# Strassen sums of the gate and up products made by TensorE inside two PSUM banks

## The chip, the cores and the metric

The kernel runs on one NeuronCore of one Trainium2 chip. The metric is device time in microseconds, the median of several executions of the whole program. Five engines take part, each with a queue of its own that it works through in order: TensorE (PE in the profile; its weight loads are PEld), VectorE (DVE), ScalarE (ACT), GpSimd (POOL) and SyncE (SP), which issues most of the loads and stores.

## The reference

```python
h   = x + irfft2(rfft2(layernorm(x)) * (w_r + 1j * w_i))       # x: 2048 x 640
z   = layernorm(h)
out = h + ((z @ w_gate) * (z @ w_up)) @ w_down                  # 640 -> 1728 -> 640
```

All of it is fp32. The change lies in the last line, in `z @ w_gate` and `z @ w_up`.

## The kernel before

The first 180 us are the spectral part (transforms as matmuls, the filter, the way back), which the change leaves alone. The rest is the feed-forward part. The 2048 tokens are worked in two blocks of 1024 (`blk` 0 and 1). The 1728 columns of gate and up are cut into 14 chunks of 128; chunks 0 to 11 go through `strassen`, chunks 12 and 13 through the plain `gu` and `gate_parts`. A block runs step `p = 6` first (chunks 12 and 13, and the operands of the Strassen products), then `p = 0` to `5`, with two chunks each: an even one (`ci == 0`) and an odd one (`ci == 1`).

A chunk computes a 2 x 2 block product: rows are gate and up, columns are the block's two halves of 512 tokens (`sb`), and the first four of the five slices of 128 along the 640 are its inner pair; the fifth slice comes as an extra term. Strassen's scheme makes seven products of it in place of eight. Each value is split into a high and a low fp32r part, and `triple` issues three matmuls of 128 x 128 x 512 for each term, so the 18 terms of a chunk are 54 matmuls. The operands on the token side are `b11`, `b21`, `b22` (slices as they are, high and low part in `xt`), and the sums `t1`, `t2` (tile `TJ["12"]`), `t3` (in `ht`'s memory) and `t4` (in `xt`), which `turn_lo`, `t_rest`, `t12` and `t34` make once per block. The weights of a chunk are `wa` (as loaded) and `ws` (sums).

Before the change each product has a PSUM bank of its own (`single()`, four banks under the tag `e`; a bank is taken at the first write and is free when its last reader is done). VectorE adds the products: `p1` is the first product, copied out by ScalarE, `u2` is o6 + p1, `u3` is u2 - o7, then `u2` gains o5 (line 805), `c22` is o5 + u3, and o3 and o4 are finished in their own banks. The finished gate and up of a half are multiplied (lines 811, 825), and ScalarE writes the high part of `h` (lines 812, 826) and VectorE the low part (lines 815, 829) for the down product. In an even chunk the down product of the step before is dealt out between the gate/up products: `some(n)` issues n of its eight token tiles (`down`: 12 matmuls of 128 x 128 x 320 into one of two banks pairs `y`, 10 where the step before is `p = 6`, and one VectorE add into `x`, line 507). `some` also pops one piece of the second block's layer norm (`fill`) with each.

The next chunk's weights are made inside the current one by `prep`: `copies` (ScalarE's 1024-wide high part of `wa`, line 699, GpSimd's low part, line 700), `sums` (GpSimd, lines 703 to 706), `high` (ScalarE, line 711) and `low` (GpSimd, line 716). `load_raw` (line 688) loads the weights after those, when `low` is done with the staging tile. `issue(wdn)` makes the two parts of the down weights (lines 462, 463). `side` holds work that is hung into a chunk at `at(0)` to `at(5)`; in block 0's last chunk (11) it makes the plain chunks' weights (`at(1)`, line 462) and normalises the eight token tiles of block 1 on ScalarE (`at(2)`, line 524), which TensorE then transposes at the start of block 1's `p = 6`.

The order in each queue is written out by hand (`tc.manual_schedule()`): an engine works in the order of the calls.

```python
order = [6, 0, 1, 2, 3, 4, 5]
steps = [(blk, p) for blk in range(2) for p in order]
# end of p == 6: the last plain chunk, then what stands ahead of chunk 0 in each queue
gu(NC - 2, 1)
gate_parts(NC - 2, 1, s12)()
for f in t34(1):
    f()
issue(wdn)
```

Of the kernel before, what the change touches and what calls it, by code (L numbers as in the profile page):

```python
# [13 lines left out]
AF = mybir.ActivationFunctionType  # L14
OP = mybir.AluOpType

P = 128
# [12 lines left out]
def view(t, offset, dims):  # L30
    return bass.AP(tensor=t.tensor, offset=t.offset + offset, ap=[list(t.ap[0])] + [list(d) for d in dims])


def f32(ap):
    return ap.bitcast(F32)
# [11 lines left out]
def tile_spectral_glu(ctx: ExitStack, tc: tile.TileContext, x, wf, wgu, wlast, wdown, wdlast,  # L47
# [8 lines left out]
    tt, act = nc.vector.tensor_tensor, nc.scalar.activation  # L56
# [9 lines left out]
    def bank(tag, bufs=2):  # L66
        return pools["a"].tile([P, 512], F32, tag=tag, name=tag, bufs=bufs)
# [4 lines left out]
    def single():  # L72
        return bank("e", 4)

    def wk(shape, name):
        return work.tile(shape, F32, tag="wk", name=name)
# [4 lines left out]
    def mmx(o, l, r, start, stop):  # L81
        nc.tensor.matmul(o, l, r, start=start, stop=stop, skip_group_check=True)  # L82
# [3 lines left out]
    def pop(n=1):  # L86
        for _ in range(n):
            if fill:
                fill.popleft()()
# [9 lines left out]
    def cut(t, o, *shape):  # L99
        v = t[:, o:o + int(np.prod(shape))]  # L100
        names = [f"d{i}" for i in range(len(shape))]
        return v.rearrange(f"p ({' '.join(names)}) -> p {' '.join(names)}", **dict(zip(names[1:], shape[1:])))
# [439 lines left out]
    TJ = {}  # L542
# [28 lines left out]

    def t_rest(j):
        b = TJ["b"][:, j].rearrange("p (a k) n -> p a (k n)", a=2)
        tt(b, b, view(TJ[j], 256, [[0, 2], [1, 256]]), op=OP.subtract)

    def t12(j):
        hi, lo = (TJ["12"][:, l].rearrange("p m k n -> p (m k) n")[:, :, j * P:(j + 1) * P] for l in range(2))
# [82 lines left out]
    for t in range(NT):  # L660
# [12 lines left out]
        if t == NT - 3:  # L673
            ht = home("qm", [P, 8192], "ht", F32R)
            hts, t3 = cut(ht, 0, 3, 2, 2, 512), cut(ht, 6144, 2, 2, 512)
# [41 lines left out]

        return copies, sums, high, low

    def triple(o, terms):  # L720
        n = len(terms)
        for i, (w, a, m) in enumerate(terms):
            whi, wlo = w[:, 0, a:a + P], w[:, 1, a:a + P]
            mmx(o, whi, m[0], i == 0, False)
            mmx(o, whi, m[1], False, False)
            mmx(o, wlo, m[0], False, i == n - 1)

    def operand(sb, k):
        return xt[:, sb, k, 0], xt[:, sb, k, 1]
# [37 lines left out]
    def strassen(c, blk, slot, ahead, downs, side):  # L767
        wa, ws = W[c]

        def some(n):  # L770
            for _ in range(n):
                if downs:
                    downs.pop(0)()
                    pop(1)

        def at(n):
            for f in side.get(n, ()):
                f()

        b11, b21, b22 = ([operand(sb, k + i) for i in range(2)] for sb, k in ((0, 0), (0, 2), (1, 2)))  # L780
        t1, t2 = ([(TJ["12"][:, 0, m, k], TJ["12"][:, 1, m, k]) for k in range(2)] for m in range(2))
        t4 = [operand(1, k) for k in range(2)]
        b5 = [operand(sb, 4) for sb in range(2)]
        hh, hl = ([hts[:, slot, sb, l] for sb in range(2)] for l in range(2))

        def product(w, a, ms, extra=()):
            o = single()
            triple(o, [(w, a + P * i, m) for i, m in enumerate(ms)] + list(extra))
            return o

        o1 = product(wa, 384, b11)
        p1, u2 = wk([P, 512], "p1"), wk([P, 512], "u2")
        act(p1, o1, AF.Copy)
        o6 = product(ws, 0, t2)
        at(0)
        if ahead:
            ahead[0]()
            ahead[1]()
        tt(u2, o6, p1, op=OP.add)  # L799
        at(1)  # L800
        o7 = product(ws, 640, [(t3[:, k, 0], t3[:, k, 1]) for k in range(2)])
        u3, c22 = wk([P, 512], "u3"), wk([P, 512], "c22")
        tt(u3, u2, o7, op=OP.subtract)
        o5 = product(ws, 256, t1, [(wa, 896, b5[1])])
        tt(u2, o5, u2, op=OP.add)  # L805
        tt(c22, o5, u3, op=OP.add)
        some(2)
        at(2)
        o3 = product(ws, 896, b22, [(ws, 512, b5[1])])
        tt(o3, o3, u2, op=OP.add)  # L810
        tt(o3, o3, c22, op=OP.mult)  # L811
        act(hh[1], o3, AF.Copy)  # L812
        at(3)
        some(1)
        tt(hl[1], o3, f32(hh[1]), op=OP.subtract)
        some(1)
        o2 = product(wa, 0, b21, [(wa, 256, b5[0])])
        if ahead:
            ahead[2]()
            ahead[3]()  # L820
        tt(p1, o2, p1, op=OP.add)
        o4 = product(wa, 640, t4, [(wa, 896, b5[0])])
        some(1)
        tt(o4, o4, u3, op=OP.add)
        tt(o4, o4, p1, op=OP.mult)  # L825
        act(hh[0], o4, AF.Copy)  # L826
        at(4)
        some(2)
        tt(hl[0], o4, f32(hh[0]), op=OP.subtract)
        some(8)  # L830
        at(5)

# [4 lines left out]
    for n, (blk, p) in enumerate(steps):  # L837
        if p == 6:
            s13, s12 = count % 3, (count + 1) % 3
            if blk == 0:  # L840
# [16 lines left out]
                for j in range(4):  # L857
                    t_rest(j)
# [8 lines left out]
            else:  # L867
# [21 lines left out]
                for j in range(4):  # L889
                    t1s[j][0]()  # L890
                    t_rest(j)
# [25 lines left out]
        for ci in range(2):  # L917
            c = 2 * p + ci
            side = {}
            ahead = None  # L920
            if c < 11:
                ahead = prep(c + 1, blk)
                side[5] = [lambda c=c: load_raw(c + 2)] if c < 10 else []
            if ci == 0:
                side[3] = [lambda wdn=wdn: issue(wdn)]
            if c == 11 and blk == 0:
                pop(len(fill))
                dj = load_direct(1, [wk([P, D], "draw"), stage[:, 0:640], stage[:, 640:1280]])
                side[1] = [lambda: issue(dj[0]), lambda: issue(dj[1]), lambda: load_raw(0)]

                def low(ks):
                    for k in ks:
                        if k == 0:
                            TJ["z"] = home("qr", [P, 6, D], "zt")
                        normalise(8 + k, TJ["z"][:, k] if k < 6 else wk([P, D], "z"))

                side[2] = [lambda: low(range(8))]
            strassen(c, blk, slots[ci], ahead, downs if ci == 0 else [], side)
            count += 1
# [134 lines left out]
```

## Time and profile before

| | us |
|---|---|
| median of 3 runs | 723.58 (723.57 to 725.05) |
| profiled execution, span from first to last instruction | 723.0 |
| of it TensorE busy | 703.4 |
| VectorE busy | 467.6 |
| ScalarE busy | 252.6 |
| GpSimd busy | 293.3 |
| mean granted TensorE clock | 0.993 of full speed |

The span is that of one profiled execution; the median of the runs is 0.6 us above it. In the timeline, instructions of one kind that follow each other are merged into a row, with their count at the end; a bracket gives the engine's idle time before the row and what ended it. L82 is the one line that issues all matmuls of the feed-forward part, so they are told apart by their tiles: `e<-xt,wst`, `e<-t,wst` and `e<-ht,wst` are gate/up products of the Strassen chunks, `e<-xt,wdir` those of the plain chunks, `y<-wd,ht` the down product.

### The profile page before, as it was taken

The page shows a single profiled execution, that of the slowest core. Times are in us where ns is not written, and L with a number is a line of the kernel's source. Part 1 is how long each engine was busy: PE and PEld are TensorE (multiplying, and loading weights), DVE is VectorE, ACT ScalarE, POOL GpSimd, SP SyncE. Part 2 cuts the span into 40 slices and gives each one's busy share as a digit, 9 for nine tenths or more (in the row PEclk, how much of TensorE's full clock was granted, in tenths as well). Part 3 has the DMA queues.
Part 4 walks back from the last instruction along what each step waited for, and adds up shares of the span by engine and source line. Part 5 has one row for each costly group of instructions (what it writes and reads, how often), then busy time and mean ns, then how long its engine had stood idle before and what let it go on. Part 6 is the DMA issues. An engine that isn't in the chain of part 4 may idle for free.

```text
span 723.0 us, 10130 instructions
## 1 busy us (share of the span) xinstructions
PE 703.4 (97%) x3892; PEld 624.1 (86%) x3892; DVE 467.6 (65%) x810; ACT 252.6 (35%) x481; POOL 293.3 (41%) x270
## 2 busy tenths in 40 slices
PE   7899998999999999999999999999999999999998
PEld 7888997987878898989898888888898989898987
DVE  7968887698976665656555557565555555555454
ACT  4756666355532222122222256232222221222200
POOL 3310114332144545546464624055545446464600
PEclk9899999999999999999999999999999999999999
DMA  9405765000221212121010222311212121110203
GB/s 339 166 1 163 232 203 192 1 0 1 73 74 37 73 37 73 37 73 38 19 65 26 92 74 92 127 37 37 73 36 74 38 73 36 37 63 10 73 1 146
DMA packets 20928, 55.06 MB, mean 76 GB/s; under 512 B 2320, under 2 KB 6928, under 8 KB 20880
## 3 DMA queue, kind: packets, MB, share of 16 engines
q1 hardware_dynamic: 20304, 52.70, 21.4%
q0 software_dynamic: 288, 1.48, 0.6%
q8 instruction: 31, 0.51, 0.3%
q10 hardware_dynamic: 288, 0.23, 0.1%
q14 instruction: 17, 0.14, 0.1%
HBM read 49.16 MB, written 5.24 MB: 75 GB/s over the span
## 4 chain that ended last, share of the span: by engine, by line
PE 82%; DVE 11%; issue 4%; ACT 2%; DMA 1%; POOL 0%; DVEq 0%; POOLq 0%; ACTq 0%
PE e L82 43%; PE y L82 26%; PE re L82 2%; PE im L82 2%; PE u L340 2%; PE eo L82 2%; DVE fold L190 2%; DVE fold L195 1%; DVE x L507 1%; PE im L389 1%; PE im L390 1%; PE ir L381 1%; ACT zt L524 1%; DVE bits L214 1%; DVE x L509 1%
## 5 line engine op out<-in xcount | busy, mean ns | idle before, releaser
L82 PE MATMUL e<-xt,wst 128*128 128x512 f32 x864 | 207.0, 390 | 0.9 <-DVE ht L653 0.9
L82 PE MATMUL y<-wd,ht 128*128 128x320 f32 x1312 | 201.7, 310 | 1.6 <-DVE x L507 1.1
L82 PEld LDWEIGHTS y<-wd,ht 128*128 128x128 f32 x1312 | 195.3, 188 | 6.4 <-DVE x L507 2.7
L82 PEld LDWEIGHTS e<-xt,wst 128*128 128x128 f32 x864 | 160.6, 188 | 32.9 <-DVE ht L653 1.3
L507 DVE TENSOR_TENSOR x<-y,x 128x640 f32<-128x640 f32 x119 | 97.7, 822 | 73.6 <-PE y L82 73.3
L700 POOL TENSOR_TENSOR wst<-raw,wst 128x1024 fp32r<-128x1024 f32 x24 | 58.0, 2418 | 168.5 <-ACT wst L699 168.5
L716 POOL TENSOR_TENSOR wst<-raw,wst 128x896 fp32r<-128x896 f32 (+1 forms) x46 | 64.9, 1433 | 22.3 <-ACT wst L711 22.3
L82 PE MATMUL e<-t,wst 128*128 128x512 f32 x288 | 73.2, 389 | 0.0
L463 POOL TENSOR_TENSOR wd<-draw,wd 128x640 fp32r<-128x640 f32 x28 | 44.4, 1607 | 56.9 <-ACT wd L462 42.5
L812 ACT ACTIVATE ht<-e 128x512 fp32r<-128x512 f32 x24 | 14.4, 599 | 151.3 <-DVE e L811 151.3
L82 PEld LDWEIGHTS e<-t,wst 128*128 128x128 f32 x288 | 54.0, 188 | 11.7 <-ACT u L650 0.5
L826 ACT ACTIVATE ht<-e 128x512 fp32r<-128x512 f32 x24 | 14.4, 599 | 114.0 <-DVE e L825 114.0
L82 PE MATMUL e<-xt,wdir 128*128 128x512 f32 x180 | 41.9, 391 | 1.1 <-DVE q L493 1.1
L82 PEld LDWEIGHTS e<-xt,wdir 128*128 128x128 f32 x180 | 33.4, 188 | 8.3 <-ACT xt L546 1.3
L699 ACT ACTIVATE wst<-raw 128x1024 fp32r<-128x1024 f32 x24 | 25.4, 1060 | 33.8 <-DMA raw<-in_wgu_dram 33.8
L206 PE MATMUL im<-bits,fold 128*128 128x128 f32 x192 | 30.9, 306 | 6.1 <-DVE fold L195 1.8
L82 PE MATMUL e<-ht,wst 128*128 128x512 f32 x144 | 36.5, 389 | 0.0
L805 DVE TENSOR_TENSOR u<-e,u 128x512 f32<-128x512 f32 x24 | 16.6, 692 | 29.5 <-PE e L82 29.4
L206 PEld LDWEIGHTS im<-bits,fold 128*128 128x128 f32 x192 | 26.6, 209 | 9.5 <-POOL fold L180 4.2
L799 DVE TENSOR_TENSOR u<-e,p 128x512 f32<-128x512 f32 x24 | 16.6, 692 | 24.0 <-PE e L82 23.0
L408 POOL CAST qr<-bits 1x128 fp32r<-1x128 f32 x16 | 4.5, 282 | 68.0 <-DVE qr L405 68.0
L82 PEld LDWEIGHTS e<-ht,wst 128*128 128x128 f32 x144 | 27.0, 188 | 5.6
(185 smaller groups left out, 1049.2 us busy)
## 6 DMA issues: line engine op xcount, KB each, us to landing
raw<-in_wgu_dram SPq DMA_DIRECT2D x24, 640.0 KB, 3.9
wts<-in_wf_dram SPq DMA_DIRECT2D x16, 644.0 KB, 4.1
draw<-in_wdown_dram SPq DMA_DIRECT2D x24, 320.0 KB, 4.7
x<-in_x_dram SPq DMA_DIRECT2D x16, 320.5 KB, 5.9
out_dram<-x SPq DMA_DIRECT2D x15, 320.0 KB, 2.2
bits<-in_mm_dram SPq DMA_DIRECT2D x32, 128.0 KB, 4.1
raw<-in_wgu_dram SPq DMA_DIRECT2D x4, 320.0 KB, 4.2
draw<-in_wdlast_dram SPq DMA_DIRECT2D x4, 320.0 KB, 2.9
```

What stands on the lines that cost most here:

```text
L82: nc.tensor.matmul(o, l, r, start=start, stop=stop, skip_group_check=True)
L190: lambda: nc.vector.scalar_tensor_tensor(view(f, 320, [[161, 2], [1, 161]]), view(XP[t], 0, [[320, 2], [1, 161]]), SC[t][1], view(XP[t], 6 ...
L206: nc.tensor.matmul(pm[:, k * P:(k + 1) * P], l, c, start=n == 0, stop=n == len(ls) - 1)
L340: nc.tensor.matmul(ps[h][:, 0:NQ], WM[g][0][:, h], T[g][:, h], start=True, stop=True)
L463: los.append(lambda r=r, a=a, b=b: engine.tensor_tensor(w[:, 1, a:b], r, f32(w[:, 0, a:b]), op=OP.subtract))
L507: tt(xv, ps[:, :, 0:320], xv, op=OP.add)
L699: act(wa[:, 0], stage[:, 0:1024], AF.Copy)
L700: nc.gpsimd.tensor_tensor(wa[:, 1], stage[:, 0:1024], f32(wa[:, 0]), op=OP.subtract)
L716: ptt(ws[:, 1, o:o + b - a], stage[:, a:b], f32(ws[:, 0, o:o + b - a]), op=OP.subtract)
L799: tt(u2, o6, p1, op=OP.add)
L805: tt(u2, o5, u2, op=OP.add)
L812: act(hh[1], o3, AF.Copy)
```

## The change

The seven products stay, and so do their 54 matmuls; the signs of the `t3` operand are turned (`t_rest` makes d - b for the first half of the tile and b - d for the second, in two half-size VectorE operations instead of one). Three banks per chunk are named at its start: `p11`, `acc_a` and `p53`. In `acc_a` the products b11, t2, t3 and t4 are accumulated one after the other (`start=False` leaves what is in the bank), and what stands there between them is read out: ScalarE copies b11's product to `p1` and the sum with t2 to `u2`, VectorE adds the sum with t3 to `m5`, and after t4 the bank holds the finished sum. In `p53` the t1 product is copied to `m5` by ScalarE and b22 is added on top. The product of b21 moves from the sixth to the second place. VectorE's operations fall from eleven to seven per chunk, ScalarE's rise from three to five (without the weights). The down steps of an even chunk, two, two and four before, become two, one, two and three.

```diff
@@ -571,7 +571,9 @@
 
     def t_rest(j):
         b = TJ["b"][:, j].rearrange("p (a k) n -> p a (k n)", a=2)
-        tt(b, b, view(TJ[j], 256, [[0, 2], [1, 256]]), op=OP.subtract)
+        d = TJ[j][:, 2:4].rearrange("p k n -> p (k n)")
+        tt(b[:, 0], d, b[:, 0], op=OP.subtract)
+        tt(b[:, 1], b[:, 1], d, op=OP.subtract)
 
     def t12(j):
         hi, lo = (TJ["12"][:, l].rearrange("p m k n -> p (m k) n")[:, :, j * P:(j + 1) * P] for l in range(2))
@@ -717,11 +719,11 @@
 
         return copies, sums, high, low
 
-    def triple(o, terms):
+    def triple(o, terms, start=True):
         n = len(terms)
         for i, (w, a, m) in enumerate(terms):
             whi, wlo = w[:, 0, a:a + P], w[:, 1, a:a + P]
-            mmx(o, whi, m[0], i == 0, False)
+            mmx(o, whi, m[0], start and i == 0, False)
             mmx(o, whi, m[1], False, False)
             mmx(o, wlo, m[0], False, i == n - 1)
 
@@ -783,50 +785,47 @@
         b5 = [operand(sb, 4) for sb in range(2)]
         hh, hl = ([hts[:, slot, sb, l] for sb in range(2)] for l in range(2))
 
-        def product(w, a, ms, extra=()):
-            o = single()
-            triple(o, [(w, a + P * i, m) for i, m in enumerate(ms)] + list(extra))
-            return o
-
-        o1 = product(wa, 384, b11)
-        p1, u2 = wk([P, 512], "p1"), wk([P, 512], "u2")
-        act(p1, o1, AF.Copy)
-        o6 = product(ws, 0, t2)
+        p11, acc_a, p53 = single(), single(), single()
+
+        def product(o, w, a, ms, extra=(), start=True):
+            triple(o, [(w, a + P * i, m) for i, m in enumerate(ms)] + list(extra), start)
+
+        product(acc_a, wa, 384, b11)
+        p1, u2, m5 = (wk([P, 512], n) for n in ("p1", "u2", "m5"))
+        act(p1, acc_a, AF.Copy)
+        product(p11, wa, 0, b21, [(wa, 256, b5[0])])
         at(0)
         if ahead:
             ahead[0]()
             ahead[1]()
-        tt(u2, o6, p1, op=OP.add)
+        tt(p1, p11, p1, op=OP.add)
         at(1)
-        o7 = product(ws, 640, [(t3[:, k, 0], t3[:, k, 1]) for k in range(2)])
-        u3, c22 = wk([P, 512], "u3"), wk([P, 512], "c22")
-        tt(u3, u2, o7, op=OP.subtract)
-        o5 = product(ws, 256, t1, [(wa, 896, b5[1])])
-        tt(u2, o5, u2, op=OP.add)
-        tt(c22, o5, u3, op=OP.add)
+        product(acc_a, ws, 0, t2, start=False)
+        act(u2, acc_a, AF.Copy)
+        product(p53, ws, 256, t1, [(wa, 896, b5[1])])
+        act(m5, p53, AF.Copy)
         some(2)
         at(2)
-        o3 = product(ws, 896, b22, [(ws, 512, b5[1])])
-        tt(o3, o3, u2, op=OP.add)
-        tt(o3, o3, c22, op=OP.mult)
-        act(hh[1], o3, AF.Copy)
+        product(acc_a, ws, 640, [(t3[:, k, 0], t3[:, k, 1]) for k in range(2)], start=False)
+        tt(m5, acc_a, m5, op=OP.add)
+        some(1)
+        product(p53, ws, 896, b22, [(ws, 512, b5[1])], start=False)
+        tt(p53, p53, u2, op=OP.add)
+        tt(p53, p53, m5, op=OP.mult)
+        act(hh[1], p53, AF.Copy)
         at(3)
-        some(1)
-        tt(hl[1], o3, f32(hh[1]), op=OP.subtract)
-        some(1)
-        o2 = product(wa, 0, b21, [(wa, 256, b5[0])])
+        some(2)
+        tt(hl[1], p53, f32(hh[1]), op=OP.subtract)
         if ahead:
             ahead[2]()
             ahead[3]()
-        tt(p1, o2, p1, op=OP.add)
-        o4 = product(wa, 640, t4, [(wa, 896, b5[0])])
+        product(acc_a, wa, 640, t4, [(wa, 896, b5[0])], start=False)
         some(1)
-        tt(o4, o4, u3, op=OP.add)
-        tt(o4, o4, p1, op=OP.mult)
-        act(hh[0], o4, AF.Copy)
+        tt(acc_a, acc_a, p1, op=OP.mult)
+        act(hh[0], acc_a, AF.Copy)
         at(4)
-        some(2)
-        tt(hl[0], o4, f32(hh[0]), op=OP.subtract)
+        some(1)
+        tt(hl[0], acc_a, f32(hh[0]), op=OP.subtract)
         some(8)
         at(5)
```

## Rows read from the trace of the kernel before

**Rows 1.** The page's busy us, share of the span and instructions of TensorE.

```profile
PE 703.4 (97%) x3892; PEld 624.1 (86%) x3892; DVE 467.6 (65%) x810; ACT 252.6 (35%) x481; POOL 293.3 (41%) x270
```

**Rows 2.** The chain of waits (start us, us, what), one pair of chunks.

```profile
267.67 18.39 PE e L82 x81
...
286.05 3.52 PE y L82 x24
```

**Rows 3.** Timeline, block 0's first chunk: start us, us, engine, line, operation.

```profile
202.90 1.65 PE L82 MATMUL e<-xt,wst 128*128 128x512 f32 x6 [0.88 <-DVE ht L653]
...
203.97 0.58 ACT L650 ACTIVATE u<-e 128x512 f32<-128x512 f32 x1
...
206.86 1.35 ACT L462 ACTIVATE wd<-draw 128x640 fp32r<-128x640 f32 x2
...
208.12 0.59 ACT L793 ACTIVATE p<-e 128x512 f32<-128x512 f32 x1
...
211.24 2.02 PE L82 MATMUL y<-wd,ht 128*128 128x320 f32 x12 [0.37 <-POOL wd L463]
...
213.10 2.23 PE L82 MATMUL e<-xt,wst 128*128 128x512 f32 x9
...
227.19 1.74 PE L82 MATMUL y<-wd,ht 128*128 128x320 f32 x10 [0.44 <-DVE x L507]
```

**Rows 4.** Timeline, first chunk of block 1, same columns.

```profile
475.01 1.52 PE L82 MATMUL e<-xt,wst 128*128 128x512 f32 x6
...
476.01 0.60 ACT L652 ACTIVATE ht<-e 128x512 fp32r<-128x512 f32 x1 [2.06 <-DVE e L651]
...
478.71 0.59 ACT L793 ACTIVATE p<-e 128x512 f32<-128x512 f32 x1
...
497.76 1.47 PEld L82 LDWEIGHTS y<-wd,ht 128*128 128x128 f32 x10 [0.31 <-DVE x L507]
```

**Rows 5.** Timeline, last chunk of block 0 and block change, same columns.

```profile
421.99 1.55 PE L82 MATMUL e<-xt,wst 128*128 128x512 f32 x6
...
427.65 4.99 ACT L524 ACTIVATE zt<-x,b,r 128x640 f32<-128x640 f32 x6 [1.60 <-PE e L82]
...
434.17 0.58 ACT L812 ACTIVATE ht<-e 128x512 fp32r<-128x512 f32 x1
...
437.44 0.60 ACT L826 ACTIVATE ht<-e 128x512 fp32r<-128x512 f32 x1 [2.69 <-DVE e L825]
...
441.51 2.02 PE L82 MATMUL y<-wd,ht 128*128 128x320 f32 x12 [0.50 <-DVE x L507]
```

**Rows 6.** Timeline of VectorE ahead of block 0's first chunk; line 803's group.

```profile
196.93 0.43 DVE L706 TENSOR_TENSOR raw<-raw 128x256 f32<-128x256 f32 x1
...
197.28 2.49 DVE L574 TENSOR_TENSOR bt<-bt,tj 128x512 f32<-128x512 f32 x4
...
L803 DVE TENSOR_TENSOR u<-u,e 128x512 f32<-128x512 f32 x24 | 16.5, 688 | 14.3 <-PE e L82 13.7 <-POOL wd L463 0.5
```

**Rows 7.** Timeline, an odd chunk and the next's start; GpSimd's line 716.

```profile
267.51 1.55 PE L82 MATMUL e<-xt,wst 128*128 128x512 f32 x6
...
278.88 2.82 POOL L716 TENSOR_TENSOR wst<-raw,wst 128x896 fp32r<-128x896 f32 x2 [2.21 <-ACT wst L711]
...
281.44 0.60 ACT L826 ACTIVATE ht<-e 128x512 fp32r<-128x512 f32 x1 [2.33 <-DVE e L825]
...
L716 POOL TENSOR_TENSOR wst<-raw,wst 128x896 fp32r<-128x896 f32 x23 | 48.8, 2124 | 22.3 <-ACT wst L711 22.3
```

**Rows 8.** Stretches: us, busy us (instructions) by engine, granted clock, DMA share, GB/s.

```profile
120.00:125.00 5.00, 2.90 (x21) 2.13 (x19) 3.76 (x9) 3.04 (x8) 2.59 (x6) 1.00 0.12 46
...
125.00:130.00 5.00, 4.61 (x22) 4.64 (x22) 1.01 (x3) 0.44 (x1) 1.23 (x4) 0.66 0.00 0
...
202.00:203.00 1.00, 0.12 (x2) 0.11 (x1) 1.00 (x3) 0.00 (x0) 0.00 (x0) 1.00 0.75 113
```

## The prediction

> **What bounds the kernel now.** I read the page's busy times first: TensorE is busy for 703.4 of the 723.0 us span [rows 1], so an edit can win only where TensorE stands still, and lose wherever it makes TensorE wait. The chain of waits says the same for the Strassen part: for pages on end it names TensorE alone. There 81 gate/up matmuls take 18.39 us, 0.227 each, and 24 down matmuls 3.52, 0.147 each [rows 2]. A pair of chunks (108 of the first, 96 of the second) is 38.6 us with no gap, and neither VectorE nor ScalarE stands on that chain. Then I read the timeline at the seams, where TensorE does wait: the first Strassen chunk of each token block [rows 3, 4], the change from block 0 to block 1 [rows 5], and the spectral part, which the change does not touch.
>
> **The change, part by part.**
>
> *Matmuls.* Seven products before and after, 18 terms of 3 matmuls, 54 in all. TensorE's work stays, so in the steady part the gain is nil. Per chunk VectorE loses four of its eleven operations (0.688 us each [rows 6], 24 x 4 x 0.688 = 66 us) and ScalarE gains two copies (0.59 each, as the one that is there [rows 3]; 28 us). VectorE is not on the chain, so its 66 us buy nothing by themselves.
>
> *New waits in a steady chunk.* TensorE now adds into a bank that ScalarE or VectorE has just read, four times per chunk, and all its later matmuls queue behind each wait. A copy starts about 0.2 us after its product and takes 0.6, so 0.8 us are needed. The product put between has at least 6 matmuls, 1.36 us, so about 0.5 us is to spare. What can use it up is ScalarE's queue. At the start of an even chunk the first copy stands behind the activation that ends the odd chunk before it; that activation starts at 281.44 today [rows 7], the copy 0.5 later. Its multiply now comes after the other half's subtraction, but one add is gone, so both start some 0.05 us later; the copy is done at 282.6, and the third product starts at 279.80 + 15 x 0.2275 = 283.2 (279.80 is 54 matmuls after the chunk's start [rows 7]). Covered by 0.6.
>
> *The moved weights.* The products that end the first half of h move from the 36th to the 45th matmul of an odd chunk, 2.05 us later; behind that activation in ScalarE's queue stand the high parts of the next weights, behind those GpSimd's low parts, behind those SP's next weight load, behind that the next 1024-wide weight copy. GpSimd's low part starts at 278.88 and its first piece lasts 2.12 [rows 7]; it becomes 280.93 to 283.05. Its reader, the third matmul of the sum product, moves as well, from the 9th matmul of the next chunk to the 18th: 283.67. Before and after some 0.6 us (0.4 if the weights are wanted one matmul ahead). The load lands about 2 us later and holds the u copy to 289.2, while two down steps put its reader at 290.1. I take 0 for the 24 steady chunks.
>
> The Trainium skill (Perfetto Trace Analysis, section Matmuls) speaks against this change: independent matmul groups should rotate through different banks, so that the copy out of one overlaps the next group. By that alone all four waits of 0.8 would be bare, 24 x 4 x 0.8 = 77 us by the rows; the product put between them is why I do not take it.
>
> *First chunk of block 0.* Here ScalarE is late. In its queue ahead of the first product's copy stand the gate parts of chunk 12, a T34 activation and two weight activations; the copy runs from 208.12 to 208.71, 5.2 us after the first matmul at 202.90 [rows 3]. Nobody minded: the first bank was wanted only by the fifth product. Now the third product wants it after 15 matmuls, 3.4 us. VectorE feeds this queue (TensorE's own wait at 202.90 is for it), and it gets eight half-size subtractions for four: 2.49 us become 8 x 0.35 = 2.8 by the spacing of the 256-wide operations at 196.93 and 197.28, at most 8 x 0.43 = 3.4 [rows 6]. So +0.3 (0 to 0.95). Then: first product 203.20 to 204.57; second product in the bank whose reader ended at 204.56, now 204.86, so 204.9 to 206.95; copy done at 209.0; third product 209.1; 30 matmuls done at 209.1 + 15 x 0.2275 = 212.5, two down steps (20 x 0.147) 215.45. Today 27 matmuls and the two steps are done at 213.10 [rows 3], with three more 213.8. Loss 1.7. This has already swallowed the 0.37 wait for the down weights at 211.24, since the first down step comes 3 matmuls later. Against it the 0.44 wait at 227.19 goes: there two down steps' adds, an add, a multiply and a third add were in one row on VectorE, of which the add leaves and the down steps are spread; with the refilling of the weights 0.5. Net +1.2.
>
> *First chunk of block 1.* The same queue: first matmul at 475.01, copy at 478.71 to 479.30; its head, the activation at 476.01, waits for the last product before, so it can't be earlier [rows 4]. The third product would start at 478.42; it waits until 479.35, with the weights' refill 1.0 us. VectorE's extra 0.3 is hidden, since it waits for TensorE here. The 0.31 wait at 497.76 goes. Net +0.7.
>
> *Block change.* In block 0's last chunk ScalarE normalises eight tiles, from 427.65 [rows 5], as soon as the T operands were read. Now two copies come before them: the second can start 0.2 after 30 matmuls, 421.99 + 6.83 + 0.2 = 429.0, so the eight start at 429.5. They last 6.5 (434.17 - 427.65), so h's first activation moves from 434.17 to 436.0. After it: subtraction 0.7, one multiply 0.7 (it was add, add, multiply), second activation at 438.05 instead of 437.44. All transposed copies follow it, then the down step's add that TensorE waits for at 441.51: +0.6. Bounds 0 (something else is late by as much) and 1.85 (the whole delay).
>
> *End.* The last chain is add, multiply, activation, subtraction; now the first half's chain ends 2.05 us nearer the end, and multiply, activation and subtraction of the second follow. By the same durations it ends within 0.1 us. 0.
>
> Sum: 1.2 + 0.7 + 0.6 = 2.5 us on the profiled span of 723.0, 725.5. The median of the runs, 723.58, lies 0.6 above that span: **726.1 us**, 0.35% slower.
>
> **The rivals.**
> 1. *The clock falls.* From 120 to 125 us TensorE stood idle for 2.1 of 5 us in short gaps; from 125 to 130 its granted clock was 0.66 on the mean, that is 3.4 us at its lower level, 1.2 GHz, and 1.7 lost [rows 8]. In block 0's first chunk it would now stand idle 1.2, 0.3 and 2.1 us within 7. For it: about as idle a stretch. Against: today's 0.88 wait at 202 left the clock at 1.00 [rows 8]. 726.1 + 1.7 = 727.8. The Trainium skill (TensorE: Matmul & The Clock Gate, section on psum-queue depth-cycling) describes it: short idles between matmul groups, caused by cycling through banks, make the clock swing.
> 2. *Odd chunks miss their weights.* The 0.4 us to spare is the only cover where an odd chunk is followed by an even one, 10 times. If the new copies push the low parts back by 0.3 more than that, 10 x 0.3 = 3.0: 729.1.
> 3. *Banks are handed out in strict turn.* Then the second product of a chunk gets the bank that the chunk before reads last (the activation at 281.44 and a subtraction behind it, 282.8) and not at 281.2: 10 x 1.6 = 16, 742. Against: at 202.90 the first product waits for the gate bank of chunk 12, which is the bank freed longest ago and not the next in turn.
> 4. *Not slower: the block starts are covered.* If ScalarE reaches the first copy within 3.4 us of the first matmul, neither wait appears, and what is left is -0.37 - 0.44 - 0.31 + 0.6 = -0.5: 723.1. It decides at that one point. For: nothing but the written order puts four activations ahead. Against: the rows show them in that order in both blocks, at 3.7 and 5.2 us.
> 5. *Faster.* As 4, and the remaining waits at the seams go too (0.88 at 202.90, 0.50 at 441.51 instead of +0.6): 721.1. Nothing in the rows speaks for it.
>
> **How the numbers follow.** Chances: forecast 0.46 (own range 725.1 to 727.2, from the bounds of the subtractions and of the block change), clock 0.22, weights 0.08, banks 0.03, covered 0.14, faster 0.07. A measurement can tell about 0.2%, 1.45 us: 722.1 to 725.0 counts as the same. Slower: 0.46 x 0.92 + 0.22 + 0.08 + 0.03 = 0.75; same 0.18; faster 0.07. The range leaves out the faster case, the banks, most of the weights and a little of the covered case: 724.0 to 728.8.
>
> **What would show it.** Right: the steady pair still 38.6 us; a wait of TensorE for ScalarE's first copy of about 2 us near 207 and 1 us near 478; the waits at 211.24, 227.19 and 497.76 gone; the wait at 441.5 about 0.6 later; VectorE's busy time down by some 65 us, ScalarE's up by 28. Wrong: waits for a copy or for low parts in every second chunk (rivals 2, 3), a granted clock of 0.5 near 209 (rival 1), or a first copy that comes before the 15th matmul (rival 4).

## The result and the profile after

The changed kernel takes 727.17 us (median of 7 runs, 725.52 to 727.35); the kernel before, run beside it, 723.85 (723.41 to 725.11). The ratio over all runs is 1.0035, 95% interval 1.0024 to 1.0047: slower by about a third of a per cent, as forecast, at a forecast of 726.1 us. The times of both kernels lie in two groups some 1.6 us apart (before 723.4 to 723.9 and 725.1, after 725.5 to 725.9 and 727.2 to 727.4), and as the median before fell into the lower group and the median after into the upper, the 3.3 us between the medians overstate the change, which costs 2.1 to 2.2 us group by group. Stage by stage, by the starts of matmuls in the two traces (stage A's start is that of its row in the timeline, the others are the chain's, which lie 0.16 us behind the row in both kernels):

| stage | begins with | before us | after us | difference | forecast |
|---|---|---|---|---|---|
| A: end of block 0's `p = 6` and its first Strassen chunk | 45 plain-chunk matmuls at 191.53; 190.00 | 37.40 | 38.46 | +1.06 | +1.2 |
| B: ten steady chunks of block 0 | 228.93; 228.46 | 193.22 | 193.20 | 0.0 | 0 |
| C: chunk 11 and the block change | 422.15; 421.66 | 32.59 | 33.11 | +0.52 | +0.6 |
| D: block 1's `p = 6` and first chunk | 454.74; 454.77 | 44.76 | 45.53 | +0.77 | +0.7 |
| E: ten steady chunks of block 1 | 499.50; 500.30 | 193.10 | 193.20 | +0.1 | 0 |
| F: last chunk and end | 692.60; 693.50 | 30.4 | 30.3 | -0.1 | 0 |

A, C and D make 2.35, forecast 2.5. The page of the changed kernel, against [rows 1]: VectorE 61 us less (467.6 to 406.5), ScalarE 27 more (252.6 to 279.3), TensorE the same work.

```profile
PE 701.4 (97%) x3892; PEld 620.4 (86%) x3892; DVE 406.5 (56%) x722; ACT 279.3 (39%) x529; POOL 293.0 (40%) x270
```

The chain of waits of the changed kernel, one pair of steady chunks, which answers to [rows 2]:

```profile
228.46 19.07 PE e L82 x84
...
261.82 5.28 PE y L82 x36
267.10 19.07 PE e L82 x84
```

The pair is 267.10 - 228.46 = 38.64 us, as before, with TensorE alone on the chain. Where TensorE waits in the feed-forward part is seen in the list of its waits (waiting line, releaser's line, us in total, times, longest):

```profile
PE e L82 <- ACT p L795: 2.6, 2, 1.8
...
PE e L82 <- DVE ht L655: 1.2, 1, 1.2
...
PE y L82 <- DVE x L507: 1.0, 1, 1.0
...
PE y L82 <- ACT ht L815: 0.5, 1, 0.5
```

These are the lines that bear on the change: two waits for the first product's copy (line 795), none for the other two new copies (804, 806) in the 24 chunks of this execution; the wait for the down weights [rows 3] and those at 227.19 and 497.76 [rows 3, 4] are not in the list any more. The timeline of block 0's first chunk, against [rows 3]:

```profile
201.64 4.03 PE L82 MATMUL e<-xt,wst 128*128 128x512 f32 x15 [1.16 <-DVE ht L655]
...
204.16 0.60 ACT L654 ACTIVATE ht<-e 128x512 fp32r<-128x512 f32 x1 [0.87 <-DVE e L653]
204.66 1.05 ACT L586 ACTIVATE xt<-bt 128x1024 fp32r<-128x1024 f32 x1
...
205.60 1.35 ACT L462 ACTIVATE wd<-draw 128x640 fp32r<-128x640 f32 x2
...
206.86 0.58 ACT L795 ACTIVATE p<-e 128x512 f32<-128x512 f32 x1
...
207.49 3.06 PE L82 MATMUL e<-t,wst 128*128 128x512 f32 x12 [1.82 <-ACT p L795]
```

ScalarE works without a pause from 204.16 to the copy: T34's activation and the down weights' two stand ahead of it, and the third product waits 1.82 us. In block 1, against [rows 4], the same, with 0.78:

```profile
478.74 0.59 ACT L795 ACTIVATE p<-e 128x512 f32<-128x512 f32 x1
...
479.37 3.02 PE L82 MATMUL e<-t,wst 128*128 128x512 f32 x12 [0.78 <-ACT p L795]
```

The block change, against [rows 5]:

```profile
428.58 0.60 ACT L806 ACTIVATE m<-e 128x512 f32<-128x512 f32 x1 [1.50 <-PE e L82]
429.07 4.98 ACT L524 ACTIVATE zt<-x,b,r 128x640 f32<-128x640 f32 x6
...
435.58 0.58 ACT L815 ACTIVATE ht<-e 128x512 fp32r<-128x512 f32 x1
...
436.21 1.28 PE L82 MATMUL y<-wd,ht 128*128 128x320 f32 x6 [0.53 <-ACT ht L815]
...
436.80 0.69 DVE L824 TENSOR_TENSOR e<-e,p 128x512 f32<-128x512 f32 x1
...
437.52 0.60 ACT L825 ACTIVATE ht<-e 128x512 fp32r<-128x512 f32 x1 [1.36 <-DVE e L824]
...
441.59 2.02 PE L82 MATMUL y<-wd,ht 128*128 128x320 f32 x12 [1.03 <-DVE x L507]
```

The normalisations stand behind the copy of line 806, and h's first activation, behind them, is late. Part of this comes back before h's second activation (line 825, before the change 826): in the kernel before, two adds stood between them on VectorE, beside a subtraction and a multiply that both kernels have. They were

```profile
435.39 0.68 DVE L821 TENSOR_TENSOR p<-e,p 128x512 f32<-128x512 f32 x1
435.99 0.69 DVE L824 TENSOR_TENSOR e<-e,u 128x512 f32<-128x512 f32 x1
```

### The profile page after: what moved, and what is told of

The parts are those of the page before. It is cut to its first block, busy times and chain, and to the rows that moved or that the text cites. A ratio compares the mean times of both kernels' runs of the same rounds, so it can differ in the third digit from the quotient of the medians.

```text
span 723.8 us, 10024 instructions
## 1 busy us (share of the span) xinstructions
PE 701.4 (97%) x3892; PEld 620.4 (86%) x3892; DVE 406.5 (56%) x722; ACT 279.3 (39%) x529; POOL 293.0 (40%) x270
## 4 chain that ended last, share of the span: by engine, by line
PE 81%; DVE 13%; ACT 3%; issue 2%; DMA 1%; DVEq 0%; ACTq 0%
PE e L82 42%; PE y L82 27%; PE re L82 2%; PE im L82 2%; PE u L340 2%; PE eo L82 2%; DVE fold L190 1%; DVE fold L195 1%; PE im L389 1%; PE im L390 1%; PE ir L381 1%; ACT zt L524 1%; DVE bits L214 1%; DVE x L509 1%; DVE q L492 1%
## 5 line engine op out<-in xcount | busy, mean ns | idle before, releaser
L82 PE MATMUL e<-xt,wst 128*128 128x512 f32 x864 | 209.2, 390 | 1.2 <-DVE ht L655 1.2
L82 PE MATMUL e<-t,wst 128*128 128x512 f32 x288 | 69.5, 390 | 2.6 <-ACT p L795 2.6
L810 DVE TENSOR_TENSOR m<-e,m 128x512 f32<-128x512 f32 x24 | 16.6, 691 | 54.7 <-PE e L82 54.3
L801 DVE TENSOR_TENSOR p<-e,p 128x512 f32<-128x512 f32 x24 | 16.6, 692 | 39.5 <-PE e L82 38.5
L813 DVE TENSOR_TENSOR e<-e,u 128x512 f32<-128x512 f32 x24 | 16.8, 700 | 29.1 <-PE e L82 29.1
```

Of the source, the lines that this page charges most:

```text
L801: tt(p1, p11, p1, op=OP.add)
L810: tt(m5, acc_a, m5, op=OP.add)
L813: tt(p53, p53, u2, op=OP.add)
```

## The experiments

**1. The down weights behind the copy.** Is it ScalarE's order that costs, at the two first chunks? The first hunk is the end of `p == 6`.

```diff
-            issue(wdn)
+            held = wdn
...
+                if p == 0:
+                    side[0] = [lambda held=held: issue(held)]
```

> The changed kernel, but in the first chunk of each block ScalarE makes the two down weight parts after the first product's copy instead of before it. Theory (the loss at the first chunks is the place of that copy in ScalarE's queue): the copy comes 1.3 us earlier. Block 0: TensorE's wait for it falls from 1.82 to about 0.5 us; block 1: from 0.78 to nothing. Sum -2.2 us against the changed kernel, ratio to the kernel before 1.0005 instead of 1.0035. The down weights are ready at about 210.4 by the time of the changed kernel's trace, their reader comes at 210.9, so no wait there. Rival (the wait belongs to the bank sharing itself, not to the queue): the waits stay, ratio 1.0035.

Measured: 723.36 us (12 runs), ratio 0.9997 (0.9988 to 1.0006). Stage A is 37.18 us (from 38.46), D 44.45 (from 45.53), 2.36 us together where 2.2 were expected; B and C stay (193.20, 33.12). The copy now comes at 205.68, right behind T34's activation:

```profile
205.68 0.59 ACT L795 ACTIVATE p<-e 128x512 f32<-128x512 f32 x1
...
206.16 1.36 ACT L462 ACTIVATE wd<-draw 128x640 fp32r<-128x640 f32 x2
...
206.32 1.89 PE L82 MATMUL e<-t,wst 128*128 128x512 f32 x7 [0.57 <-ACT p L795]
```

The wait falls from 1.82 to 0.57, and A by 1.28; the one of 0.78 in block 1 is gone, and D is 1.08 shorter. It is ScalarE's order, and the wait that goes altogether, block 1's, gives back 0.3 us more than the list shows for it (experiments 4 and 6 say the same).

**2. VectorE makes the copies in chunk 11 of block 0.** Is the block change late because of the two copies ahead of the normalisations?

```diff
+        copy = nc.vector.tensor_copy if (blk, c) == (0, 11) else lambda o, i: act(o, i, AF.Copy)
...
-        act(u2, acc_a, AF.Copy)
+        copy(u2, acc_a)
...
-        act(m5, p53, AF.Copy)
+        copy(m5, p53)
```

> The changed kernel, but in block 0's chunk 11 the copies u2 and m5 are made by VectorE, so that ScalarE can start normalising when the T operands were read. Theory: the eight normalisations start about 1.5 us earlier (near 427.6 where they start at 429.07), h's first activation near 434.1 instead of 435.58, and TensorE's wait before the third down step at the block change falls from 1.03 to about 0.5 us; -0.5 us in all, ratio 1.0028. That is less than the timing can tell, so the trace decides. Rival (another chain holds that down step): its wait stays near 1.0 although the normalisations start earlier.

Measured: 724.59 us (11 runs), ratio 1.0018 (1.0009 to 1.0028). Stage C is 31.88: 1.23 us less than the change's 33.11, where 0.5 were expected, and 0.7 less than before's 32.59. The timeline:

```profile
427.86 4.99 ACT L524 ACTIVATE zt<-x,b,r 128x640 f32<-128x640 f32 x6 [2.23 <-PE e L82]
...
434.38 0.58 ACT L816 ACTIVATE ht<-e 128x512 fp32r<-128x512 f32 x1
...
436.32 0.60 ACT L826 ACTIVATE ht<-e 128x512 fp32r<-128x512 f32 x1 [1.36 <-DVE e L825]
...
440.38 1.88 PE L82 MATMUL y<-wd,ht 128*128 128x320 f32 x11 [0.74 <-DVE x L507]
```

The normalisations start 1.21 earlier than in the changed kernel, and the end of the stage moves by all of it: the place was right and the size was not. TensorE's wait for line 507 falls only to 0.74, but the one of 0.53 before it is gone as well. The end of the stage hangs on h's second activation: the row in which TensorE waits for line 507 starts 4.07, 4.07 and 4.06 us after it in the kernel before, the changed kernel and here. Counted from the start of chunk 11 (421.99, 421.50 and 421.51), h's first activation starts at 12.18, 14.08 and 12.87, the second at 15.45, 16.02 and 14.81. So the change delays the first by 1.90 us, 1.2 of it by the two copies and 0.7 because the T operands' last product now ends three matmuls later; the two adds that VectorE no longer makes in between give back 1.33, and 0.57 is left. With the copies on VectorE, the second activation comes 0.64 earlier than before, and C is 0.71 shorter.

**3. The old scheme at the seams alone.** Chunk 0 of both blocks and chunk 11 of block 0 in the scheme of before, the other 21 in the new one; the turned sign of `t3` and with it the half-size subtractions stay.

```diff
+    def strassen_apart(c, blk, slot, ahead, downs, side):
...
+        tt(u3, u2, o7, op=OP.add)
...
-            strassen(c, blk, slots[ci], ahead, downs if ci == 0 else [], side)
+            scheme = strassen_apart if c == 0 or (blk, c) == (0, 11) else strassen
+            scheme(c, blk, slots[ci], ahead, downs if ci == 0 else [], side)
```

> The changed kernel, but chunk 0 of both blocks and chunk 11 of block 0 keep seven products in banks of their own, in the old order; the other 21 chunks accumulate in two banks. Theory (all of the loss lies at these three seams): TensorE's waits for copies vanish, and what is left against the kernel before is the doubled half-size subtractions, 0.3 us; ratio 1.0000 to 1.0010. Rival (the steady chunks lose a little each, 21/24 of the loss): ratio about 1.003.

Measured: 723.74 us (11 runs), ratio 1.0005 (0.9996 to 1.0014). Stages A, C, D are 37.64, 32.60, 44.75 (before 37.40, 32.59, 44.76), B 193.25. The change's loss in A, C and D is that of three chunks, and the ten steady chunks of stage B cost nothing. Those of stage E cost 0.8 us in this execution (193.97, after 193.20), by one wait for a copy, which had been expected to vanish:

```profile
674.25 1.06 ACT L701 ACTIVATE wst<-raw 128x1024 fp32r<-128x1024 f32 x1 [6.70 <-DMA raw<-in_wgu_dram]
...
675.85 1.66 PE L82 MATMUL e<-ht,wst 128*128 128x512 f32 x6 [0.50 <-ACT u L804]
```

The load of the next weights was issued at 668.87 and let ScalarE begin 5.4 us later, against 3.9 to 4.7 in the nine other even chunks of B and E; the copy of `u2` stood behind it. What is left in A, 0.24 us, fits the half-size subtractions (forecast 0.3), the only part of the change that stays there.

**4. No product between.** The t2 product stands right behind b11's in the same bank, in every chunk.

```diff
         product(acc_a, wa, 384, b11)
...
         act(p1, acc_a, AF.Copy)
+        product(acc_a, ws, 0, t2, start=False)
+        act(u2, acc_a, AF.Copy)
...
-        product(acc_a, ws, 0, t2, start=False)
-        act(u2, acc_a, AF.Copy)
```

> The changed kernel, but the product that shares the first product's bank comes right behind it in every chunk, with no other product between. Theory (the product put between is what hides the copy): TensorE now waits for the copy in every chunk. Where ScalarE is free the wait is 0.2 + 0.6 + 0.05 = 0.85 us; where an even chunk follows an odd one, the copy stands behind the activation of h and the wait is about 1.5; in the first chunks of the blocks it grows by 2. 12 x 0.85 + 10 x 1.5 + 4 + the 2.6 that are there = about 30 us more than the changed kernel less these 2.6, so 753 (750 to 758). Rival (TensorE's queue hides a wait of that size): under 730.

Measured: 760.63 us in a single run, span 758.8, 35.0 above the changed kernel's; 753, that is 29.2 above its span, was expected. The list of waits and a steady chunk's row:

```profile
PE e L82 <- ACT p L795: 27.5, 24, 4.2
```

```profile
317.94 1.65 PE L82 MATMUL e<-t,wst 128*128 128x512 f32 x6 [0.69 <-ACT p L795]
...
331.68 1.77 PE L82 MATMUL e<-t,wst 128*128 128x512 f32 x6 [1.21 <-ACT p L795]
```

The 0.69 is an odd chunk's, where the copy finds ScalarE free; the 1.21 is an even one's, where the activation of line 825 stands ahead of it. Two things make the loss larger than expected. A pair loses 41.23 - 38.64 = 2.59 us where 0.85 + 1.5 = 2.35 was expected; the waits shown are only 1.90, but each costs 0.35 more than it shows. And the clock falls. Stretches of block 0's first chunk (us, busy us and count of PE, PEld, DVE, ACT, POOL, granted clock, DMA share, GB/s):

```profile
202.00:204.00 2.00, 1.44 (x6) 0.83 (x5) 1.34 (x3) 1.07 (x2) 0.00 (x0) 1.00 0.96 387
204.00:206.00 2.00, 0.00 (x0) 0.00 (x0) 1.08 (x3) 1.69 (x3) 0.00 (x0) 1.00 0.51 201
206.00:208.00 2.00, 0.36 (x1) 0.36 (x2) 1.11 (x1) 1.59 (x3) 1.45 (x1) 0.68 0.00 0
208.00:210.00 2.00, 2.00 (x6) 1.54 (x6) 0.00 (x0) 0.00 (x0) 2.00 (x2) 0.50 0.00 0
```

TensorE waits 4.2 us there; the granted clock falls to 0.50, which is 1.2 GHz, and the next 24 matmuls take 8.51 us in the chain instead of 24 x 0.2275 = 5.46. Of the 3.05 more, 0.33 is what the changed kernel's chain shows behind such a wait too (3.74 us for 15 matmuls, 3.41 at 0.2275); 2.7 are lost to the clock.

**5. All three seams mended.** Experiment 2's copies by VectorE, and both the down weights and T34's last activation (with VectorE's subtraction that belongs to it) behind the first copy.

```diff
-            for f in t34(1):
-                f()
-            issue(wdn)
+            held = t34(1) + [lambda wdn=wdn: issue(wdn)]
...
+                if p == 0:
+                    side[0] = held
```

> The changed kernel with all three seams mended: in block 0's chunk 11 VectorE makes the two copies, and both the last T34 activation and the down weights' activations are issued behind the first Strassen product's copy of each block. My theory (the loss is ScalarE's queue at three places and nowhere else): against the changed kernel 1.3 us come back at block 0's first chunk with the weights moved alone; the T34 activation moved too takes most of the 0.57 us wait that was left there (0.5); 0.7 at block 1's; 1.2 at the block change. Sum about 3.5 us off the changed kernel: 723.7 less, counted like with like against the kernel before, some 1.2 us faster than before, ratio about 0.998 (0.997 to 0.9995), and no wait of TensorE for line 795's copy in the trace. Rival (the remedies overlap, or the moved activations make the second or fourth product late instead): ratio 1.000 or above, with a new wait near 206 to 215 us or near 476 to 485 us.

Measured: 721.77 us (6 runs, 721.61 to 721.82), ratio 0.9970 (0.9958 to 0.9982) to the kernel before, which took 723.57 beside it: faster than both kernels, by 0.3% than the one before. Stages A to D are 36.79, 193.20, 31.89, 44.45. The list of TensorE's waits has no line for the three copies any more; what is left of those above is

```profile
PE e L82 <- DVE ht L655: 1.2, 1, 1.2
...
PE y L82 <- DVE x L507: 0.7, 1, 0.7
```

and there is a new wait of 0.2 us for the down weights, which now come later. The span is 720.0, 3.8 below the changed kernel's, where 3.5 were expected.

**6. The second copy three times over.** How much more would the cover bear?

```diff
-        act(m5, p53, AF.Copy)
+        for _ in range(3):
+            act(m5, p53, AF.Copy)
```

> The changed kernel with the M5 copy (the second copy out of a shared bank) done three times over in every chunk; the result is the same. It tests the size of the cover. My theory: the product put between needs 6 matmuls, 1.36 us; from the product's end to the release one copy needs 0.2 + 0.6, three need 0.2 + 0.6 + 2 x 0.49 + 0.05 = 1.83. So each chunk in which no down step stands there (12 of 24) waits 0.47 us, with the refill of the weights about 0.6, and the block change moves by about 1 us: 727.2 + 12 x 0.6 = 734, with 12 waits of about 0.5 us for line 806's copy; the other 12, which have two down steps (3.6 us) more of cover, none. Rival (ScalarE's queue, not the cover, sets what can be borne): the second copy delays the next weights' high parts as well, and waits for weights appear, 740 or more. Rival (the release is earlier than the copy's end): under 730.

Measured: 736.73 us in a single run, span 735.0, 11.2 above the changed kernel's; about 7 was expected. The waits, and the rows of an odd chunk (no down step) and of the even one behind it:

```profile
PE e L82 <- ACT m L807: 7.1, 12, 0.6
```

```profile
274.96 1.86 ACT L807 ACTIVATE m<-e 128x512 f32<-128x512 f32 x3 [1.44 <-PE e L82]
...
276.88 7.79 PE L82 MATMUL e<-xt,wst 128*128 128x512 f32 x33 [0.59 <-ACT m L807]
...
291.42 1.55 PE L82 MATMUL e<-ht,wst 128*128 128x512 f32 x6
```

Twelve waits of 0.59, in the chunks without a down step there, and none in the other twelve: as the first theory has it. The price is higher: a pair is 39.54 us instead of 38.64, so 0.90 for a wait shown as 0.59, again 0.31 more; 12 x 0.90 = 10.8, and the block change adds 0.4. With one copy the same arithmetic leaves 1.36 - 0.85 = 0.5 us of cover unused.

**7. The new order without the change.** Does the mended kernel's gain come from the change, or only from the order of ScalarE's work? The kernel before, with the edit of experiment 5 in `p == 6` and `side[0]`, and nothing else.

> The kernel before, with the last T34 activation and the down weights' activations issued behind the first Strassen product's copy, as in the mended kernel, and nothing of the change. It asks whether the 1.8 us that the mended kernel is faster than before come from the change or from the new order. My theory (from the change: its fewer VectorE operations take away waits of 0.44, 0.68 and 0.31 us for VectorE at the three seams): here those waits stay, and the down weights come 0.5 us later behind the copy, so that the wait for them of 0.37 us near 211 becomes about 0.8. 723.6 + 0.4 = 724.0, ratio 1.0005 (1.000 to 1.0015). Rival (the order gives the gain): about 721.8, ratio 0.9975, with none of the waits for VectorE left.

Measured: 724.31 us (11 runs), ratio 1.0000 (0.9991 to 1.0009). Stages A to D are 37.85, 193.21, 32.61, 44.99. The waits for VectorE stay, and those for the down weights grow (0.37 in one wait before):

```profile
208.92 1.15 PE L82 MATMUL y<-wd,ht 128*128 128x320 f32 x6 [0.25 <-POOL wd L463]
210.44 2.02 PE L82 MATMUL y<-wd,ht 128*128 128x320 f32 x12 [0.37 <-POOL wd L463]
...
226.40 1.73 PE L82 MATMUL y<-wd,ht 128*128 128x320 f32 x10 [0.44 <-DVE x L507]
```

So the order alone gains nothing: the timing shows no difference, and the stages are 0.45 (A), 0.02 (C) and 0.23 us (D) longer than before, 0.7 in all, where the down weights come later. Against before, the mended kernel gains 0.61 in A, 0.70 in C and 0.31 in D, 1.6 in all. In C it is VectorE's two adds (experiment 2), in D the wait of 0.31 for VectorE at 497.76 [rows 4] is gone. In A the wait of 0.44 for VectorE is gone and the one for the down weights, which are GpSimd's, falls from 0.37 to 0.2, while the wait for line 655 is 0.28 longer. Against this kernel the mended one gains 1.06, 0.72 and 0.54, 2.3 in all; it differs from this kernel by the change and by VectorE's copies in chunk 11, which only the change has.

## Why the prediction held

*Steady chunks, 0.* Held: the pair is 38.64 before and after, and in experiment 3 the ten of stage B cost nothing, those of stage E 0.8 in one wait behind a late weight load, which the forecast did not have. The Trainium skill (Perfetto Trace Analysis, section Matmuls) has independent groups rotate through banks; by that alone the four waits would have been bare. They are covered, because another bank's product stands between, and the copies overlap it, as the page would have it; experiment 4 shows what one of the four costs when it is bare in every chunk, 35 us with the clock's part.

*Moved weights, 0.* Held: in the changed kernel the odd chunk's low part starts 13.41 us after its chunk (280.35 - 266.94), before 11.37 [rows 7]; the 2.04 are the 2.05 of the forecast, and TensorE has no wait for them.

*First chunk of block 0, +1.2.* Measured +1.06. The third product starts at 207.49, which is 209.02 on the scale of before (the stage begins 1.53 earlier); forecast 209.1. The half-size subtractions' 0.3 is 0.24 in experiment 3 (the wait of TensorE that follows them, 0.88 before, is 1.16), and experiment 1 returns 1.28 with the weights alone.

*First chunk of block 1, +0.7.* Measured +0.77. Third product at 479.37, forecast 479.35. The wait shown is 0.78 and gives back 1.08 in experiment 1; the forecast had 0.93 and under 0.1 for refilling the weights, for which no row stood: the runs show about 0.3 behind a wait, and the two misses cancel.

*Block change, +0.6.* Measured +0.52, and the steps come where they were put: on the scale of before (0.49 later) the normalisations at 429.56 (429.5), h's first activation at 436.07 (436.0), the wait ends at 442.08 (441.51 + 0.6). The working holds too: the forecast took 1.85 of delay, less what VectorE's fewer operations give back before h's second activation (438.05 instead of 437.44); measured are 1.90, and 438.01 on the scale of before. What was mis-sized is experiment 2's expectation, which had 0.5 for the two copies; they cost 1.2.

*The median.* The sum came out well because two wrong numbers in it cancel. One is the 0.6 us between span and median. In the eight other executions profiled here the run's own time lies 1.7 to 2.0 above its span (725.52 and 723.8 in the changed kernel). The execution profiled of before held a stretch at the lower clock, between 125 and 130 [rows 8], and the changed kernel's did not: its `p = 6` rows begin 1.53 us earlier, though the change does not touch what comes before them. So the other is the span of 723.0, 1.53 too long; the runs of before at 723.6 us have spans of 721.5 to 721.7. The spans profiled, 723.0 and 723.8, differ by 0.8, and with the 1.53 added by 2.3, the sum of the stages. That the median came out at 727.17, 1.1 above the forecast, and not near 725.7 as three of the seven runs did, the forecast's terms do not explain: how close the median came is luck.

*The rivals.* Weights (2) and banks (3): no such wait in any steady chunk of the changed kernel. Covered (4) and faster (5): refuted by the two waits for line 795. The clock (1): refuted for this change, since the granted clock is 1.00 through block 0's first chunk:

```profile
202.00:204.00 2.00, 1.96 (x9) 1.31 (x8) 1.34 (x3) 1.07 (x2) 0.00 (x0) 1.00 1.01 411
204.00:206.00 2.00, 1.68 (x8) 1.03 (x6) 1.08 (x3) 1.84 (x3) 0.00 (x0) 1.00 0.39 154
206.00:208.00 2.00, 0.51 (x2) 0.46 (x3) 1.49 (x2) 2.00 (x4) 1.59 (x1) 1.00 0.02 4
208.00:210.00 2.00, 2.00 (x10) 1.59 (x10) 0.17 (x1) 0.99 (x2) 2.00 (x3) 1.00 0.04 8
```

In experiment 4's one execution, with a wait of 4.2 us at the same place, the clock fell, and at 2.7 us the price was more than the 1.7 put on it. The Trainium skill (TensorE: Matmul & The Clock Gate, section on psum-queue depth-cycling) has the clock swing with frequent short idles between groups, by which rival 1 would have come true; here the granted clock stayed at 1.00 through idles of 1.16 and 1.82 us.

## What to carry to other kernels

Several products can share a PSUM bank with copies between them at no cost, as long as another bank's product of more than copy latency plus copy (here 0.8 us) stands between and the copying engine is free; what has to be looked at is not so much the steady loop as the seams, where that engine's queue is full of other work. In the loop, look for what in its queue waits for a load: one load that came 1.2 us late cost 0.8 (experiment 3). A copy that used to be unwaited-for becomes urgent when its bank is reused at once: move it ahead of work that nobody needs yet, or to the engine that the change has relieved. The engine that the change relieves paid only at the seams as well, so count the waits for it there, not its busy time: 61 us less of VectorE came with 1.6 us less of time, once the seams were mended.

## What the runs showed of the hardware

Two things had not been expected. A wait of TensorE costs about 0.3 us more than the idle time shown: 0.90 for 0.59 (experiment 6), 2.59 for 1.90 in two waits (experiment 4), 1.08 for 0.78 (experiment 1, block 1). About half of it lies in how a row is drawn: six matmuls are a row of 1.52 us, but in the flow they take 6 x 0.2275 = 1.365, and the idle time is counted from the row's end. The rest was not pursued.

And the same busy time before a stretch was followed by the lower clock in one execution and not in others. From 120 to 126 us TensorE was busy for 3.5 us in the kernel before and in the changed one, in the same instructions; from 126 to 128 the granted clock was 0.50 in the one and 1.00 in the other, as in the seven experiments:

```profile
124.00:126.00 2.00, 0.70 (x6) 0.61 (x5) 0.70 (x2) 1.01 (x3) 0.96 (x3) 1.00 0.00 0
126.00:128.00 2.00, 2.00 (x16) 2.00 (x15) 0.00 (x0) 0.42 (x1) 0.71 (x3) 1.00 0.00 0
```

```profile
124.00:126.00 2.00, 0.70 (x5) 0.64 (x5) 0.70 (x2) 0.98 (x3) 0.99 (x3) 0.99 0.00 0
126.00:128.00 2.00, 2.00 (x10) 2.00 (x9) 0.00 (x0) 0.00 (x0) 0.69 (x3) 0.50 0.00 0
```

The first two rows are the changed kernel's, the other two those of the kernel before. It is worth 1.53 us. What decides it is open.
